# A decay table made by a scan on VectorE, fewer weight tiles decoded in the retention, and the first MLP outputs made tile by tile

## The chip, the cores and the metric

The kernel runs on one core of a Trainium2 chip. The metric is the device time of one execution in microseconds (us). TensorE, VectorE, ScalarE and GpSimd each run their own instruction list in order; the profile calls them PE (with PEld for its weight loads), DVE, ACT and POOL, and SP is the queue that issues most transfers.

## The reference, cut to what matters

Three layers run one after the other on a (2, 768, 512) activation, in float32. The MLP's weights arrive as 64-bit floats and must be decoded on the chip.

```python
# 1 retention: 8 heads of 64, blocks of 64 positions, a decay lam per head
Dmask = np.where(rel >= 0, lam[:, None, None] ** rel[None, :, :], 0.0)
intra = np.einsum('bhij,bhjd->bhid', np.einsum('bhic,bhjc->bhij', qb, kb) * Dmask[None], vb)
inter = np.einsum('bhid,bhde->bhie', qb * lam_pow[None], kv_state)
kv_state = lam_block * kv_state + np.einsum('bhsd,bhse->bhde', kb * rev_pow[None], vb)
# 2 MLP: layer norm, 512 -> 2048 -> 512, residual
xn = (x - mu) / np.sqrt(var + 1e-06) * g_ln
x = x + np.maximum(xn @ w_ch1, 0.0) @ w_ch2
# 3 attention with 4 experts, of which the gate takes 2
```

## The kernel before, in words

**Retention.** The main loop (L590) takes 12 chunks, n = 0 to 11, of 128 positions (two batches of six). Chunk n issues the scores of chunk n+1 (`ret_scores`, L322), the state products (`ret_state`, L352) and the inner products (`ret_inner`, L385). `ret_sum` (L363, L365) adds a state on DVE, twice per chunk (EARLY, then LATE), and POOL multiplies it by the decay (`old`, L375). `ret_decay` multiplies the next chunk's keys (`kd`, L337 on ACT, L338 on POOL) and scores (`a`, L341 on DVE) by the table `dec`. `ret_outer` (L402) adds the part that comes from the states, and `ret_copy` (L409) takes the chunk's result to `xT` on ACT. Scores and outputs share two large PSUM buffers (`ps_big`). Chunks with nothing else for PE run three dummy matmuls (`warm`, L100).

**The table.** `dec` is lam to the power i, for each head and position. Before, DVE makes the powers in six doublings on 8 partitions (L262), they go out to `zd` in DRAM and back in a shifted pattern to 64 partitions (L269), and ACT copies them to the other 64 (L270). The input loads of chunks 1 and 2 are issued on SP behind these transfers.

**Decoding.** One weight tile (a 512 KB load, L121, with three buffers) takes seven DVE instructions of 128x512 (L204, L205, L209, L218, L219, L223, L226) and two on ACT (L200, L214), in six parts (`prep_parts`). Each part has a hand-set cost; `room(us)` issues parts until the costs reach the budget. In the retention `room` is called twice per chunk, with 1.7 and 2.0. It takes the layer norm's parts (`minus` L439 and `low` L445 of a block of 384 positions) before weight parts. The eight tiles of group 0 (four of w1, four of w2) are decoded there.

**MLP.** There are four blocks of 384 positions and four groups of four tiles. A `g1` step is 12 matmuls (L503) and leaves `h` through a relu on ACT (L515) and a subtraction on DVE (L516). A `g2` step is 24 matmuls (L530), half of a block's output for one group, and is added to `xT` on DVE (L535). `steps` is the order, written out by hand; five `g1` steps stand in the retention, one per chunk in n = 6 to 10. After chunk 11 the by-hand loop goes on for six rounds of two steps, up to step 17. From there `mlp_step` runs one step at a time, and a planner (`plan`) says before which step a tile of groups 1 to 3 is decoded: here one per two steps from step 12. `ln_e` (L462 on PE, L484 on DVE) scales a block before its `g2`. Attention follows the MLP.

Of the kernel before, what the change touches and what calls it, by code (L numbers as in the profile page):

```python
# [17 lines left out]
P = 128  # L18
# [26 lines left out]
FIRST = ((0, 0), (1, 0), (2, 0), (0, 1), (1, 1), (2, 1), (0, 2), (1, 2), (2, 2), (3, 0))  # L45
# [18 lines left out]
def model(ctx, tc, qkT, kv, lam, g_ln, w12, wat, out):  # L64
# [69 lines left out]

    steps = [("g1", 0, blk, f) for f, blk in FIRST]
    for blk in range(NBLK - 2):
        steps += [("g2", 0, blk, 0), ("g1", 0, blk + 1, GF - 1), ("g2", 0, blk, 1)]
    groups = [(g, blk) for g in range(NG) for blk in range(NBLK)]
    for n, gb in enumerate(groups):
        if n < NBLK - 2:  # L140
            continue
        steps.append(("g2", *gb, 0))
        if n + 1 < len(groups):
            steps += [("g1", *groups[n + 1], f) for f in range(2)]
        steps.append(("g2", *gb, 1))
        if n + 1 < len(groups):
            steps += [("g1", *groups[n + 1], f) for f in range(2, GF)]

    def used(ft, i):

        at_ = [n for n, (kind, g, _, f) in enumerate(steps)
               if kind == ("g1", "g2")[i] and g == ft // GF and (i == 1 or f == ft % GF)]
        return at_[0], at_[-1]
# [7 lines left out]
    while rest:  # L161
        for p in rest:
            ft, i = p
            old = ft - W_SLOTS[i][1]
            if used(ft, i)[0] - n <= LEAD and (old < 0 or used(old, i)[1] < n - 1):
                break
        else:
            p = None
        if p and n >= free_at:
            plan[n] = p  # L170
            rest.remove(p)
            free_at = n + APART
        n += 1
        assert n < len(steps), rest
# [15 lines left out]
    def prep_parts(ft, i):  # L190
# [17 lines left out]
        def top():  # L208
# [3 lines left out]
            pool, bufs = (wpool, few) if ft % many < few else (WPOOL2[0], many - few)  # L212
# [45 lines left out]
    nc.vector.memset(zt[:, :C - 1], 0.0)  # L258
    nc.vector.memset(zt[:, C - 1:C], 1.0)
    m = 1  # L260
    while m < C:
        nc.vector.tensor_scalar(zt[:, C + m:C + 2 * m], zt[:, C:C + m], zt[:, C + m - 1:C + m], None, ALU.mult)  # L262
        m *= 2
    zd = dram.tile([H, P], F32, tag="zd", name="zd")
    nc.sync.dma_start(zd, zt)
    ret_load(*order[0], 1)

    zv = zd[:, :]
    nc.sync.dma_start(dec[:C], bass.AP(tensor=zv.tensor, offset=zv.offset, ap=[[1, C], [P, H], [1, C]]))  # L269
    nc.scalar.copy(dec[C:], dec[:C])  # L270
# [195 lines left out]
    def ln_d(blk):  # L466
# [5 lines left out]
        std = lnp.tile([P, NTB], F32, tag="std", name=f"std{blk}")  # L472
# [17 lines left out]
    HS, LAST, HXT = {}, [], []  # L490

    EXTRA = FIRST[EARLY_STEPS:] + ((GF - 1, 1),)
    assert len(EXTRA) <= 2 * HX

    def g1(g, blk, f):
# [9 lines left out]
        if g == 0 and (f, blk) in EXTRA:  # L505
            n = EXTRA.index((f, blk))
            if n % 2 == 0:
                HXT.append(ap_.tile([P, 2, 1040], F32R, tag="wa", name=f"hx{n}"))
            h = HXT[n // 2][:, :, n % 2 * TB:(n % 2 + 1) * TB]
        else:  # L510
# [45 lines left out]
    def mlp_step():  # L556
# [4 lines left out]
        decode(1 if due else 0)  # L561
        f, args, leave = step()
# [4 lines left out]
    norm_parts, weight_parts = [], [part for p in first for part in prep_parts(*p)]  # L567
# [16 lines left out]
    del pieces[:len(first)]  # L584
    ret_scores(0)
# [3 lines left out]
    norm_at, n, early = [0] * NBLK, 0, 0  # L589
    while n < len(order) or min(norm_at) < 5 or norm_parts or weight_parts:  # L590
        if n < len(order):
            if n + 3 < len(order):
                ret_load(*order[n + 3])
            ret_scores(n + 1)
            ret_state(n)
            ret_inner(n)
            ret_sum(n, EARLY)
# [3 lines left out]
        for blk in range(NBLK):  # L601
            if n >= NTB * (blk + 1) and norm_at[blk] < 5 and not (norm_at[blk] == 2 and blk not in XN) \
                    and not (norm_at[blk] == 1 and blk > 0 and norm_at[blk - 1] < 3):
                norm_parts += (ln_a, ln_b, ln_c, ln_d, ln_e)[norm_at[blk]](blk) or []
                norm_at[blk] += 1
        leave = None
        if n < len(order):
            room(ROOM[0])
            ret_sum(n, LATE)
            if n >= MLP_FROM and early < EARLY_STEPS and step_ready():  # L610
                leave = step()[2]
                early += 1
# [8 lines left out]
            room(ROOM[1] - (0.6 if leave else 0.0))  # L621
# [319 lines left out]
```

## Time and profile before

| | us |
|---|---|
| median of three runs (499.32 to 501.76) | 499.38 |
| profiled execution, own time | 499.64 |
| its span, first to last instruction | 497.9 |
| TensorE busy in the span | 471.1 |
| VectorE busy | 345.8 |
| last `ret_outer` ends | 91.2 |
| last `g2` matmul ends | 358.3 |

The own time is 1.74 us more than the span. Mean granted TensorE clock over the span is 0.973 of full speed; the lower values all stand in the first 56 us.

### The profile page before, as it was taken

Reading aid. Unit: us, or ns where it says so; the run is one execution under the profiler, and the core shown is the slowest. Engines: PE = TensorE matmul, PEld = TensorE weight load, DVE = VectorE, ACT = ScalarE, POOL = GpSimd, SP = SyncE. Lnnn points to the kernel's source line nnn. Section 1 sums busy time; section 2 is a strip of 40 time slices with the busy share of each in tenths; the row PEclk is TensorE's granted clock in tenths of the full one; section 3 lists DMA queues with packets and bytes.
Section 4 is the critical chain, followed back from the end, with each engine's and each line's share of the span. In section 5 each row is a group of like instructions: output and inputs, shape, how many; then the busy total and the mean of one; then the engine's idle time right before and its main releaser. Section 6 shows DMA issues by size and latency. Waiting matters only on the chain.

```text
span 497.9 us, 10394 instructions
## 1 busy us (share of the span) xinstructions
PE 471.1 (95%) x4231; PEld 436.3 (88%) x4231; DVE 345.8 (69%) x719; ACT 199.2 (40%) x454; POOL 99.9 (20%) x146
## 2 busy tenths in 40 slices
PE   5867999899998999999999999999999999999996
PEld 2645787799998999999999999999998889898885
DVE  2899988752699556987278995544478786677663
ACT  2335555441143122232122351221156666647672
POOL 4566455000000000000000000000025535334340
PEclk9579799999999999999999999999999999999999
DMA  6965741100123202222012231000000000100111
GB/s 214 354 214 207 257 170 45 43 1 0 43 85 128 86 5 82 84 86 84 1 42 86 86 127 43 1 1 0 1 2 0 13 32 1 43 3 22 43 41 67
DMA packets 11295, 35.41 MB, mean 71 GB/s; under 512 B 1896, under 2 KB 2160, under 8 KB 11248
## 3 DMA queue, kind: packets, MB, share of 16 engines
q1 hardware_dynamic: 10928, 34.62, 19.9%
q8 instruction: 33, 0.54, 0.4%
q10 hardware_dynamic: 288, 0.14, 0.1%
q14 instruction: 14, 0.11, 0.1%
q0 software_dynamic: 32, 0.00, 0.0%
HBM read 31.60 MB, written 3.15 MB: 70 GB/s over the span
## 4 chain that ended last, share of the span: by engine, by line
PE 76%; DVE 16%; ACT 3%; issue 2%; DMA 2%; POOL 0%; SPq 0%; DVEq 0%; ACTq 0%
PE y L530 25%; PE h L503 24%; PE pj L699 4%; PE s L779 4%; PE av L828 4%; PE o L849 3%; PE t L816 3%; PE pv L721 3%; DVE mag L204 2%; DVE w L226 1%; DVE top L223 1%; DVE xn L445 1%; DVE st L365 1%; DMA qk<-in_qkT 1%; DVE top L209 1%
## 5 line engine op out<-in xcount | busy, mean ns | idle before, releaser
L503 PE MATMUL h<-xn,w 128*128 128x384 f32 x768 | 140.9, 337 | 0.0
L503 PEld LDWEIGHTS h<-xn,w 128*128 128x128 f32 x768 | 133.3, 188 | 3.3 <-issue 2.5
L530 PE MATMUL y<-hs,w 128*128 128x384 f32 x696 | 126.2, 335 | 2.6 <-DVE hs L516 2.6
L530 PEld LDWEIGHTS y<-hs,w 128*128 128x128 f32 x696 | 121.0, 188 | 2.9 <-DVE hs L516 2.9
L515 ACT ACTIVATE hs<-h 128x384 fp32r<-128x384 f32 x58 | 28.5, 491 | 115.5 <-PE h L503 95.1
L713 POOL TENSOR_SCALAR kh<-kh 64x384 fp32r<-64x384 f32 x16 | 8.4, 525 | 292.6 <-DVE qs L707 281.0
L516 DVE SCALAR_TENSOR_TENSOR hs<-h,hs 128x384 fp32r<-128x384 f32 x58 | 32.2, 555 | 46.6 <-ACT hs L515 46.5
L535 DVE TENSOR_TENSOR xT<-xT,y 128x768 f32<-128x768 f32 x32 | 30.5, 952 | 39.5 <-PE y L530 39.5
L806 POOL TENSOR_SCALAR att<-att,c,gw 128x128 f32<-128x128 f32 (+5 forms) x48 | 35.8, 751 | 51.5 <-DVE c L803 16.3
L214 ACT CAST w<-top 128x512 fp32r<-128x512 f32 x32 | 19.9, 621 | 55.3 <-DVE top L209 55.3
L699 PE MATMUL pj<-x,wa 128*128 128x384 f32 x192 | 35.0, 337 | 0.0
L699 PEld LDWEIGHTS pj<-x,wa 128*128 128x128 f32 x192 | 33.4, 188 | 0.0
L817 ACT COPY aT<-t 128x512 f32<-128x512 f32 (+3 forms) x64 | 26.5, 442 | 11.1 <-PE t L816 10.8
L816 PE MATMUL t<-ident,att 128*128 128x128 f32 x168 | 26.2, 275 | 0.4 <-DVE qs L707 0.4
L226 DVE TENSOR_TENSOR w<-top,mag 128x512 fp32r<-128x512 f32 x32 | 23.4, 732 | 0.5
L828 PE MATMUL av<-aT,v 128*64 128x128 f32 x336 | 23.6, 280 | 0.0
L779 PE MATMUL s<-kh,qs 128*128 128x512 f32 (+3 forms) x64 | 23.2, 365 | 0.0
L219 DVE SCALAR_TENSOR_TENSOR mag<-raw,mag 128x512 f32<-128x512 uint32 x32 | 22.5, 703 | 0.8
L209 DVE SCALAR_TENSOR_TENSOR top<-raw,mag 128x512 int32<-128x512 int32 x32 | 22.4, 701 | 0.6
L223 DVE TENSOR_TENSOR top<-top,w 128x512 f32<-128x512 f32 x32 | 22.7, 711 | 0.0
L402 PEld LDWEIGHTS po<-qd,st 64*64 64x64 f32 x352 | 13.1, 153 | 10.9 <-issue 7.7
L200 ACT ACTIVATE mag<-raw 128x512 f32<-128x512 f32 x32 | 21.4, 669 | 1.1 <-DVE w L226 0.4
(119 smaller groups left out, 692.5 us busy)
## 6 DMA issues: line engine op xcount, KB each, us to landing
raw<-in_w SPq DMA_DIRECT2D x32, 512.0 KB, 3.7
qk<-in_qkT SPq DMA_DIRECT2D x12, 512.0 KB, 4.5
kvn<-in_kv SPq DMA_DIRECT2D x12, 512.0 KB, 4.8
out<-os SPq DMA_DIRECT2D x11, 256.0 KB, 2.0
rawa<-in_wat SPq DMA_DIRECT2D x3, 512.0 KB, 3.2
rawa<-in_wat SPq DMA_DIRECT2D x1, 520.0 KB, 4.2
dec<-zd SPq DMA_DIRECT2D x1, 128.0 KB, 4.9
out<-os SPq DMA_DIRECT2D x1, 128.0 KB
```

The source lines that it names most:

```text
L223: nc.vector.tensor_tensor(t["top"], t["top"], t["w"][:, 0].bitcast(F32), ALU.subtract)
L226: nc.vector.tensor_tensor(t["w"][:, 1], t["top"], t["mag"], ALU.add)
L503: nc.tensor.matmul(ph[:, :TB], w[:, wi, k, :], xn[:, xi, k, :], start=(i == 0), stop=(i == 11))
L515: LAST.append((nc.scalar.activation(h[:, 0], ph[:, :TB], AF.Relu), nc.vector.scalar_tensor_tensor(h[:, 1], ph[:, :TB], 0.0, h[:, 0].bitcas ...
L516: nc.vector.scalar_tensor_tensor(h[:, 1], ph[:, :TB], 0.0, h[:, 0].bitcast(F32), ALU.max, ALU.subtract)))
L530: nc.tensor.matmul(y[:, j, :TB], w[:, wi, e * P:(e + 1) * P], h[:, xi], start=(f == 0 and i == 0), stop=(f == GF - 1 and i == 2))
L535: nc.vector.tensor_tensor(xv, xv, y[:, :, :TB], ALU.add)
L699: nc.tensor.matmul(ps[:, :TB], w[:, wi, k, :], x2[:, xi, k, :], start=(i == 0), stop=(i == 11))
L779: nc.tensor.matmul(ps[:, c0:c1], q, kk[:, e, c0:c1], start=(i == 0), stop=(i == 1))
L806: nc.gpsimd.tensor_scalar(a[:, :n], a[:, :n], c, gw, ALU.mult, ALU.mult)
L816: nc.tensor.transpose(pt[:, (j - j0) * P:(j - j0 + 1) * P], a[:, j * P:(j + 1) * P], ident)
L828: nc.tensor.matmul(pav[e2 * HD:(e2 + 1) * HD, pr * P:(pr + 1) * P], v[:, j, e * HD:(e + 1) * HD], row["aT"][e][:, j * P:(j + 1) * P], star ...
```

## The change

- **Table.** `lq` (lam on all partitions) is loaded on SP ahead of all else. POOL makes a pattern of ones (`hit`), DVE copies it to `one`, copies `lq` to `mul`, zeroes the first column and runs one `tensor_tensor_scan` (multiply, add) over 128x512, which is `dec`. The doublings, `zd`, the transfer back and ACT's copy go. POOL's order of the first instructions is now also the written one.
- **Retention.** In chunk 0 nothing is decoded and `ret_scores(1)` stands behind `ret_inner(0)`. The budgets are 0.7 and 0.9 without a step and 1.4 and 1.6 with one. Only the w1 tiles of group 0 are in the list; the w2 tiles (`later_parts`) are appended after chunk 11, with the scaling of block 0 ahead of the last. `warm` runs in n = 0 to 4; a step may stand from n = 5 on. Worked through, the readiness rules give: no dummy and no step in n = 5 and 6, a `g1` step in each of n = 7 to 11.
- **Steps.** `next_step` takes the first ready of the steps in `FIRST`. After `FIRST` block 0's output is made by four `g2f` steps (12 matmuls, one w2 tile each, both large PSUM buffers), with `g1` of block 3 between them. Ten `g1` steps of group 1 stand ahead of group 1's first `g2` (step 36). There are 98 steps, 96 before.
- **Buffers and plan.** Early `h` tiles are put into free w1 slots of w2 (`IN_W`), `wa` buffers and the `dq` buffer. Planned decoding begins at step 20, one tile before each of steps 20 to 27, then 33, 34, 38 and on.
- **Scaling of blocks 1 to 3** (`ln_e`) is issued just ahead of each block's first `g2`.

```diff
-WARM = (10, 5)
-ROOM = (1.7, 2.0)
-ROOM_MLP = 1.6
-EARLY_STEPS = 5
-MLP_FROM = 6
-PLAN_FROM = 12
-LEAD = 12
+WARM = (8, 3)
+ROOM = ((0.7, 0.9), (1.4, 1.6))
+ROOM_MLP = 1.5
+MLP_FROM = 5
+PLAN_FROM = 20
+LEAD = 16
 APART = 2
+APART_FROM = 34
+FIRST = ((0, 0), (1, 0), (0, 1), (1, 1), (2, 0), (2, 1), (0, 2), (1, 2), (2, 2), (3, 0), (3, 1), (3, 2))
...
     steps = [("g1", 0, blk, f) for f, blk in FIRST]
-    for blk in range(NBLK - 2):
-        steps += [("g2", 0, blk, 0), ("g1", 0, blk + 1, GF - 1), ("g2", 0, blk, 1)]
+    for f in range(GF):
+        steps += [("g2f", 0, 0, f), ("g1", 0, NBLK - 1, f)]
...
+        half = len(more) // 2
+        steps += [("g2", *gb, 0)] + more[:half] + [("g2", *gb, 1)] + more[half:]
+        if gb == (0, NBLK - 1):
+            steps += [("g1", 1, 1, f) for f in range(GF)] + [("g1", 1, 2, f) for f in range(2)]
...
-    nc.sync.dma_start(zt[:, C:C + 1], lam)
-    nc.scalar.dma_start(lq, lam.rearrange("h o -> o h").to_broadcast([P, H]))
-    ret_load(*order[0], 0)
+    nc.sync.dma_start(lq, lam.rearrange("h o -> o h").to_broadcast([P, H]))
+    ret_load(*order[0])
...
-        nc.vector.tensor_scalar(zt[:, C + m:C + 2 * m], zt[:, C:C + m], zt[:, C + m - 1:C + m], None, ALU.mult)
-    nc.sync.dma_start(zd, zt)
-    ret_load(*order[0], 1)
-    nc.sync.dma_start(dec[:C], bass.AP(tensor=zv.tensor, offset=zv.offset, ap=[[1, C], [P, H], [1, C]]))
-    nc.scalar.copy(dec[C:], dec[:C])
+    nc.gpsimd.memset(hit, 0.0)
+    for a2 in range(2):
+        nc.gpsimd.affine_select(hit, hit, [[1, C]], ALU.not_equal, 1.0, base=1 - C * (a2 + 1), channel_multiplier=1)
+    nc.vector.tensor_copy(one, hit[:, None, :].to_broadcast([P, H, C]))
+    nc.vector.tensor_copy(mul, lq[:, :, None].to_broadcast([P, H, C]))
+    nc.vector.memset(mul[:, :, 0:1], 0.0)
+    nc.vector.tensor_tensor_scan(dec.rearrange("p h i -> p (h i)"), mul.rearrange("p h i -> p (h i)"),
+                                 one.rearrange("p h i -> p (h i)"), 0.0, ALU.mult, ALU.add)
...
+    def g2f(g, blk, f):
+        if f == 0:
+            YF.extend(ps_big(f"yf{j}") for j in range(2))
+        for e in range(KT):
+            for i, (wi, xi) in enumerate(PASSES):
+                nc.tensor.matmul(YF[e // 2][:, e % 2, :TB], w[:, wi, e * P:(e + 1) * P], h[:, xi],
+                                 start=(f == 0 and i == 0), stop=(f == GF - 1 and i == 2))
+        def leave():
+            if f == GF - 1:
+                for j in range(2):
+                    nc.vector.tensor_tensor(xv, xv, YF[j][:, :, :TB], ALU.add)
...
+            if todo[0] == ("g2", 0, blk, 0):
+                for _, scale in ln_e(blk):
+                    scale()
...
-    norm_parts, weight_parts = [], [part for p in first for part in prep_parts(*p)]
+    weight_parts = [part for ft in range(GF) for part in prep_parts(ft, 0)]
+    for ft in range(GF):
+        if ft == GF - 1:
+            later_parts.append((2.0, lambda: [f() for _, f in ln_e(0)]))
+        later_parts += prep_parts(ft, 1)
...
-            ret_scores(n + 1)
+            SCK[n + 1] = ps_big(f"sck{n + 1}")
+            if n > 0:
+                ret_scores(n + 1)
             ret_state(n)
             ret_inner(n)
+            if n == 0:
+                ret_scores(n + 1)
...
-            room(ROOM[0])
+            leave, early = None, ROOM[0]
+            if n >= MLP_FROM and any(ready(k, True) for k in range(len(FIRST) - len(steps) + len(todo))):
+                early = ROOM[1]
+            if n > 0:
+                room(early[0])
             ret_sum(n, LATE)
-            if n >= MLP_FROM and early < EARLY_STEPS and step_ready():
-                leave = step()[2]
-                early += 1
+            if early is ROOM[1]:
+                leave = next_step(True)
             elif n < MLP_FROM:
                 warm(3, f"c{n}")
```

## Rows read from the trace of the kernel before

**Rows 1.** The page, part 1: busy time, share of the span and instructions.

```profile
PE 471.1 (95%) x4231; PEld 436.3 (88%) x4231; DVE 345.8 (69%) x719; ACT 199.2 (40%) x454; POOL 99.9 (20%) x146
```

**Rows 2.** Windows cut at the EARLY sums: stretch, length, busy by engine, clock, DMA.

```profile
14.47:22.41 7.94, 6.13 (x118) 4.02 (x116) 7.73 (x12) 2.79 (x7) 4.16 (x4) 0.50 0.95 379
22.41:29.42 7.01, 4.60 (x133) 3.33 (x131) 6.87 (x11) 2.51 (x6) 4.43 (x4) 0.86 0.68 228
...
50.59:55.58 4.99, 4.55 (x133) 4.34 (x136) 4.85 (x11) 2.49 (x6) 1.21 (x1) 0.56 0.71 253
55.58:62.38 6.80, 6.80 (x149) 5.40 (x141) 6.23 (x11) 4.56 (x9) 3.62 (x4) 1.00 0.76 278
...
91.22:126.51 35.29, 35.29 (x219) 32.93 (x220) 17.51 (x29) 10.34 (x21) 0.00 (x0) 1.00 0.05 16
126.51:160.00 33.49, 30.89 (x179) 30.57 (x178) 29.03 (x58) 11.46 (x20) 0.00 (x0) 1.00 0.28 94
160.00:358.29 198.29, 198.29 (x1152) 198.29 (x1151) 128.36 (x212) 50.68 (x93) 0.00 (x0) 1.00 0.15 51
```

**Rows 3.** Timeline, first 15 us: start, length, engine, line, what, idle before and releaser.

```profile
3.66 0.43 POOL L280 COPY qpow<-lq 64x4 f32<-64x4 f32 x2 [0.78 <-DMA lq<-in_lam]
...
10.24 0.62 ACT L270 COPY dec<-dec 64x512 f32<-64x512 f32 x1 [7.60 <-DMA dec<-zd]
...
10.94 0.73 POOL L338 TENSOR_TENSOR kd<-kvn,dec 128x320 f32<-128x320 f32 x1 [4.43 <-ACT dec L270]
...
12.47 1.08 PE L352 MATMUL sck<-kvn,kd 64*64 64x64 f32 x32
...
14.47 0.42 DVE L363 COPY st<-sck 128x256 f32<-128x256 f32 x1 [2.89 <-PE po L385]
```

**Rows 4.** Timeline of chunks 1 to 3, 25 to 38 us.

```profile
25.39 0.69 PE L322 MATMUL sck<-qk 64*64 64x64 f32 x32 [0.68 <-ACT xT L409]
...
29.98 1.15 PE L402 MATMUL po<-qd,st 64*64 64x64 f32 x32 [2.22 <-DVE st L365]
...
31.64 0.58 ACT L409 COPY xT<-po 128x512 f32<-128x512 f32 x1
...
32.27 1.13 PE L322 MATMUL sck<-qk 64*64 64x64 f32 x32 [1.14 <-ACT xT L409]
...
34.03 1.08 PE L385 MATMUL po<-a,kvn 64*64 64x64 f32 x32
...
36.48 1.46 PE L100 MATMUL warmc<-zeros 128*128 128x512 bf16 x3
```

**Rows 5.** Groups of DVE instructions from 100 to 345 us.

```profile
L516 DVE SCALAR_TENSOR_TENSOR hs<-h,hs 128x384 fp32r<-128x384 f32 x51 | 28.3, 556 | 43.0 <-ACT hs L515 42.9
L535 DVE TENSOR_TENSOR xT<-xT,y 128x768 f32<-128x768 f32 x29 | 27.6, 952 | 31.3 <-PE y L530 31.3
L219 DVE SCALAR_TENSOR_TENSOR mag<-raw,mag 128x512 f32<-128x512 uint32 x24 | 16.6, 690 | 0.5
...
L205 DVE TENSOR_SCALAR mag<-mag 128x512 int32<-128x512 int32 x24 | 10.2, 424 | 0.4
```

**Rows 6.** One decode line in the retention (15 to 92 us): minimum/median/maximum ns.

```profile
L204 DVE TENSOR_SCALAR mag<-mag x8: 420/1482/1491, 15.4 to 80.5; 128x512 f32<-128x512 f32 x8
```

**Rows 7.** Timeline, 145 to 157 us: PE's wait in the MLP.

```profile
150.77 0.55 DVE L516 SCALAR_TENSOR_TENSOR hs<-h,hs 128x384 fp32r<-128x384 f32 x1
...
151.38 0.97 PE L530 MATMUL y<-hs,w 128*128 128x384 f32 x4 [2.60 <-DVE hs L516]
...
152.18 4.32 PE L503 MATMUL h<-xn,w 128*128 128x384 f32 x24
...
156.34 4.32 PE L530 MATMUL y<-hs,w 128*128 128x384 f32 x24
```

**Rows 8.** The chain that ended last, two pieces after the retention: start, length, what.

```profile
109.57 0.78 PE va L419 x8
...
123.75 0.67 PE sb L462 x6
```

More of the change, by code (lines that the diff above doesn't have):

```diff
@@ L135, in model @@
     steps = [("g1", 0, blk, f) for f, blk in FIRST]
-    for blk in range(NBLK - 2):
-        steps += [("g2", 0, blk, 0), ("g1", 0, blk + 1, GF - 1), ("g2", 0, blk, 1)]
+    for f in range(GF):
+        steps += [("g2f", 0, 0, f), ("g1", 0, NBLK - 1, f)]
     groups = [(g, blk) for g in range(NG) for blk in range(NBLK)]
     for n, gb in enumerate(groups):
-        if n < NBLK - 2:
+        if n == 0:
             continue
[L142 to L147, printed above, removed]
+        more = []
+        if n >= NBLK - 1 and n + 1 < len(groups):
+            more = [("g1", *groups[n + 1], f) for f in range(GF)]
+        if gb == (1, 0):
+            more = [("g1", 1, 2, f) for f in range(2, GF)]
+        elif gb == (1, 1):
+            more = []
+        half = len(more) // 2
+        steps += [("g2", *gb, 0)] + more[:half] + [("g2", *gb, 1)] + more[half:]
+        if gb == (0, NBLK - 1):
+            steps += [("g1", 1, 1, f) for f in range(GF)] + [("g1", 1, 2, f) for f in range(2)]
+    assert len(set(steps)) == len(steps)
     def used(ft, i):
         at_ = [n for n, (kind, g, _, f) in enumerate(steps)
-               if kind == ("g1", "g2")[i] and g == ft // GF and (i == 1 or f == ft % GF)]
+               if g == ft // GF and (kind == "g2" and i == 1 or kind == ("g1", "g2f")[i] and f == ft % GF)]
         return at_[0], at_[-1]
@@ L164, in model @@
             old = ft - W_SLOTS[i][1]
-            if used(ft, i)[0] - n <= LEAD and (old < 0 or used(old, i)[1] < n - 1):
+            free = used(old, i)[1] if old >= 0 else steps.index(("g2", 0, ft // 2 - 1, 1)) if i == 1 else 0
+            if used(ft, i)[0] - n <= LEAD and free < n - 1:
                 break
@@ L489, in model @@
     PASSES = ((0, 0), (1, 0), (0, 1))
-    HS, LAST, HXT = {}, [], []
-    EXTRA = FIRST[EARLY_STEPS:] + ((GF - 1, 1),)
-    assert len(EXTRA) <= 2 * HX
+    HS, LAST, HXT, HDQ = {}, [], [], []
     def g1(g, blk, f):
@@ L504, in g1 @@
                 i += 1
-        if g == 0 and (f, blk) in EXTRA:
-            n = EXTRA.index((f, blk))
+        if g == 0 and (f, blk) in IN_W:
+            h = wpool.tile([P, 2, 512], F32R, tag="w1", name=f"hw{f}_{blk}", bufs=W_SLOTS[1][0])[:, :, :TB]
+        elif (ft, blk) in IN_WA:
+            n = IN_WA.index((ft, blk))
             if n % 2 == 0:
@@ L509, in g1 @@
             h = HXT[n // 2][:, :, n % 2 * TB:(n % 2 + 1) * TB]
+        elif (ft, blk) in IN_DQ:
+            n = IN_DQ.index((ft, blk))
+            if n == 0:
+                HDQ.append(xnp.tile([P, 2, KT, TB], F32R, tag="dq", name="hdq", bufs=1))
+            h = HDQ[0][:, :, n]
         else:
@@ L561, in mlp_step @@
         decode(1 if due else 0)
+        for blk in range(1, NBLK):
+            if todo[0] == ("g2", 0, blk, 0):
+                for _, scale in ln_e(blk):
+                    scale()
         f, args, leave = step()
@@ L573, in room, with ready, next_step @@
             us -= cost
-    def step_ready():
-        f, g, blk, k = todo[0]
+    def ready(k, inside):
+        f, g, blk, j = todo[k]
         if f == "g1":
-            return blk in XN and (g * GF + k, 0) in W
-        return blk in SCALED and all((g * GF + j, 1) in W for j in range(GF))
+            return blk in XN and (g * GF + j, 0) in W and not (inside and (j, blk) in IN_WA)
+        return f == "g2f" and (g * GF + j, 1) in W and (j < GF - 1 or blk in SCALED) and not inside
+    def next_step(inside):
+        for k in range(max(1, len(FIRST) - len(steps) + len(todo))):
+            if ready(k, inside):
+                return step(k)[2]
+        return None
     by_hand = ExitStack()
@@ L620, in model @@
             ret_copy(n)
-            room(ROOM[1] - (0.6 if leave else 0.0))
+            if n > 0:
+                room(early[1])
         if n == len(order) - 1:
```

54 lines of the change are left out of this document (30 added, 24 removed).

## The prediction

> **What bounds the kernel now.** I read the page first. TensorE is busy for 95% of the span [rows 1], which looks like a kernel with nothing left but matmuls. An average hides stages, so next I cut the span at the places where `ret_sum` closes a chunk [rows 2]. From 91.22 us to the last `g2` at 358.29 PE is busy for all but the 2.60 us of one wait (35.29 of 35.29, 30.89 of 33.49, 198.29 of 198.29): that stage is bound by PE. The retention is another matter. There DVE is busy for nearly all of a chunk (7.73 of 7.94, 6.87 of 7.01), PE for some two thirds, and PE's busy time contains dummies and matmuls at a lowered clock (0.50 in one chunk, 0.56 in another, 1.00 from 55.58 on). So the retention is as long as DVE's list. Five `g1` steps stand in it, before and after the change. Whatever shortens it therefore pulls the whole PE-bound stage forward, unless DVE then fails to keep up behind it.
>
> The timeline of the start [rows 3] shows the other wait: lam is on all partitions at 3.66, but ACT waits 7.60 us for `dec` to come back from DRAM, POOL's `kd` starts at 10.94 and the first sum at 14.47.
>
> **The change, part by part.** Times before are those of the profiled execution (499.64 us, which is 0.26 above the median of 499.38).
>
> *Start.* The trace has no scan. Its nearest row is a DVE instruction of 128x512, 0.69 [rows 5]; far off on the other side is the same width held up by another engine, 1.49 [rows 6]. I take 1.0, and 0.5 and 0.1 for the copy of lam and the zeroing, so the table stands at 3.7 + 1.6 = 5.3 (4.9 to 5.8). POOL's three small pattern instructions lie in its wait for lam. The table is then not what comes last: SP now issues the loads without a wait between them, and they run one behind the other. The busiest chunk moved 379 GB/s [rows 2], so 512 KB take 1.4 us. Counted from lam's landing at 3.7, the first keys land at 5.1, the first values at 6.5, then chunk 1 at 7.9 and 9.3, one weight load, and chunk 2's keys at 12.1. `kd` takes 0.73 from 6.5, state and inner products 2.0 (12.47 to 14.47), so the first sum is at 9.2, 5.3 us earlier [rows 3]. The second needs chunk 2's keys, at 12.1, and three PE groups of 2.84 (32.27 to 35.11 at the lowered clock [rows 4]): 14.9, where it was 22.41. **Term 1: -7.5.** Bounds: -5.3 if the second sum wins nothing over the first, -10.0 if lam does not hold up the loads (1.4) and the three groups take 1.7, by the 0.69 against 1.13 of one of them [rows 4].
>
> *Chunks 1 to 6.* From 22.41 to 62.38 before: 39.97, or 6.66 each, set by DVE [rows 2]. A tile is four DVE instructions of 0.69 and three of 0.42, 4.0, and 4.2 with the gaps [rows 5]; beside POOL it costs more, as one of them took 1.48 there against 0.42 [rows 6]. The new budgets leave about half a tile or half a block's norm per chunk. With the table's product (as wide as those 0.69) and two sums of 0.42 [rows 3] DVE has 3.5 to 5.1 of work. Then the chain through PE matters: dummies (the sum hidden behind them), `ret_outer`, ACT's copy, three PE groups. At the lowered clock this is 1.46 + 1.15 + 0.65 + 2.84 = 6.1, with the dummies and the three groups at the full one 0.73 + 1.15 + 0.65 + 1.7 = 4.2 [rows 4]. I take 5.1, between them and near the one chunk of before in which DVE was not held up by POOL, 4.99 at a clock of 0.56 [rows 2]: 30.6. **Term 2: -9.4**, bounds -3.4 (6.1) and -14.6 (4.2).
>
> *Chunks 7 to 11.* In 7 to 10 DVE has the two normalized blocks as before, and the decode that stands beside them is about what scaling and decode were. I put nothing for these four, within 3 either way. In chunk 11 a `g1` step of 2.08 (half of 4.16 from 152.18 to 156.34 [rows 7]) now stands in front of `ret_outer`; the step it replaces stood in chunk 6, whose time is already in term 2. **Term 3: +1.7.** The retention then ends at 91.2 - 15.2 = 76.0.
>
> *Scaling of blocks 0 and 1* leaves the retention: 2 x 0.67 of PE [rows 8] move into the PE-bound stage. **Term 4: +1.3.** `g2f` has as many matmuls as the two `g2` halves that it replaces; its two additions are the old ones.
>
> *Decode moved behind the retention.* Four w2 tiles leave it, and the planned tiles come one per step at 20 to 27 where it was one per two. I added both engines up from the end of `ret_outer(11)` to step 36, the first that needs group 1's w2. PE: 25 steps of 12 matmuls x 2.08 = 52.0 (seven left of `FIRST`, four of block 3, four `g2f`, ten of group 1), six of 24 x 4.16 = 25.0 [rows 7], four scalings x 0.67 = 2.7, six pieces of the norms at about 0.7 = 4.3 [rows 8]: 84.0. DVE: twelve tiles x 4.2 = 50.4, 21 subtractions x 0.56 = 11.8, eight additions and eight scalings x 0.95 = 15.2, a block's norm 2 x 0.95 + 4 x 0.56 = 4.1 [rows 5]: 81.5. So DVE may idle for 2.5 us; each further one is a wait of PE. Before, the same two engines stood at 30.89 and 29.03 of 33.49, and PE waited 2.60 [rows 2]: a subtraction stood behind decoding in DVE's list until 150.77, and the `g2` that needed it came at 151.38 [rows 7]. Right behind the retention DVE will wait for relus of steps that PE has still to do; I estimate 7.5 us of idle time up to step 36, so 5.0 of waits in place of 2.6. **Term 5: +2.4**, bounds -2.6 (no wait is left) and +9.
>
> The sum: -7.5 - 9.4 + 1.7 + 1.3 + 2.4 = -11.5, so 488.1, or 487.9 beside the median. Forecast 488.
>
> What is costed at nothing: SP no longer waits between its first loads, and no later load is late, since chunk 4's is issued two chunks ahead and a chunk and a half of weight moves 1.5 MB in 5 us, under the 379 GB/s of before. Steps 36 to 53 have 54 of PE against 48 of DVE by the same prices, so no wait grows there. Attention is untouched.
>
> **The rivals.** *The clock stays low.* PE's clock fell to 0.50 and 0.56 in chunks in which it was busy for 77% and 91% with short groups [rows 2], and the change drops the dummies in chunks 5 and 6. If chunks 1 to 6 run at 6.1 and the first `g1` step takes twice its 2.08: 499.6 - 7.5 - 3.4 + 1.7 + 1.3 + 2.4 + 2.1 = 496. Against it: a shorter chunk holds the same matmuls, so PE idles less. The Trainium skill (TensorE: Matmul & The Clock Gate, "HAM oscillation") says that waits between groups of matmuls can put the clock back to half each time; the low chunks here agree, and by that rule alone this rival's 496 would stand. Chance 0.14.
>
> *POOL takes DVE's place.* POOL is busy 4.43 of a chunk of 7.01, waits for DVE's sums in between, and none of its work goes [rows 2]. If it holds chunks 1 to 6 at 6.66, only the start is won: 499.6 - 7.5 + 5.4 = 497.5. Against it: 1.21 of POOL in the chunk of 4.99 (the batch's last, which has less for it), and 3.62 in chunk 6 [rows 2]. Chance 0.08.
>
> *Slower: DVE becomes the bound of steps 20 to 27.* There DVE has eight tiles, six additions, two subtractions and three scalings, 46.1, against 31.2 of PE. If the two large PSUM buffers, which come free only by DVE's additions, let PE run no further ahead, 14.9 are lost and not made good, on top of the 5.0: 499.6 - 13.9 + 19.9 - 2.6 = 503. It decides from a wait of 16.5 us on. For it: DVE's list is fixed, and it has put decoding ahead of a subtraction before [rows 7]. Against it: steps 28 to 35 need only 4.5 of DVE for 16.6 of PE, so most of a backlog is worked off. Chance 0.06.
>
> *Better:* the full clock in chunks 1 to 6 and no waits behind them, 499.6 - 7.5 - 14.6 + 3.0 - 2.6 = 478. Chance 0.14. That the change does not do what it says is no case here: the table's wait goes with the transfer.
>
> **How the numbers follow.** The forecast, 483 to 494, has 0.58. The range, 480 to 496.5, takes in the clock rival and the upper half of the better case; left out are the other half of that (0.06), POOL's and the slower case (0.14). A measurement of this kernel tells no difference under 0.5%, 2.5 us. Faster: 0.58 + 0.14 + 0.14 = 0.86; within: POOL's 0.08; slower: 0.06.
>
> **What would show it.** The first sum near 9, the second near 15; sums some 5 us apart in chunks 1 to 6; `ret_outer(11)` at 76; from there to the last `g2` 271 us, with PE waiting some 5 us for DVE between steps 20 and 36; attention 139.6 as before. The prediction is wrong if the chunks' pitch stays above 6, if loads of chunk 2 or 3 land late, or if PE waits more than 12 us behind the retention.

## The result, and the profile after

The changed kernel takes 487.97 us in the median (485.91 to 489.12), beside 500.2 for the kernel before in the same comparison: ratio 0.9748 [0.9701, 0.9794]. The forecast was 488.0 in 480 to 496.5. The profiled execution has a span of 486.8, 11.1 less than before. Its total is what was forecast; most of its terms are not.

The page of the changed kernel, part 1 (it answers to [rows 1]) and the queue from part 3 that brings the instructions (packets, MB, share):

```profile
PE 465.2 (96%) x4219; PEld 432.4 (89%) x4224; DVE 337.4 (69%) x715; ACT 198.0 (41%) x453; POOL 99.4 (20%) x149
...
q8 instruction: 33, 0.54, 0.5%
```

The changed kernel in windows, as in [rows 2]: chunk 0 from its first sum on, three of chunks 1 to 6, chunks 1 to 6 and 7 to 11 in one row each, the stage behind the retention, attention.

```profile
12.09:16.68 4.59, 3.29 (x114) 2.30 (x115) 1.45 (x4) 1.86 (x5) 3.12 (x4) 1.00 1.02 413
16.68:23.77 7.09, 3.62 (x130) 2.94 (x131) 5.54 (x9) 1.93 (x5) 3.90 (x4) 0.98 0.60 222
23.77:31.30 7.53, 5.11 (x134) 4.02 (x137) 3.67 (x8) 1.87 (x5) 4.03 (x4) 0.73 0.77 271
41.40:44.86 3.46, 2.89 (x132) 2.73 (x136) 3.25 (x6) 2.87 (x7) 1.25 (x2) 1.00 0.82 240
...
16.68:50.47 33.79, 24.03 (x766) 17.94 (x772) 24.07 (x39) 14.68 (x36) 21.40 (x22) 0.90 0.67 234
50.47:81.23 30.76, 27.61 (x600) 23.44 (x596) 25.56 (x44) 18.45 (x39) 14.01 (x16) 1.00 0.32 106
81.23:346.90 265.67, 265.67 (x1558) 263.31 (x1559) 186.98 (x323) 76.12 (x141) 0.00 (x0) 1.00 0.18 58
346.90:486.80 139.90, 135.25 (x1053) 120.13 (x1051) 96.20 (x301) 83.72 (x224) 52.86 (x80) 1.00 0.07 24
```

In the retention DVE is no longer busy for nearly all of a chunk: 24.07 of 33.79, where [rows 2] had 6.87 of 7.01. No other engine has taken its place: PE has 24.03, POOL 21.40. A stretch in which nobody is full is set by a chain of waits. Behind the retention PE is busy without a break, 265.67 of 265.67; the wait in [rows 7] is gone.

Cut at the same places as the prediction's terms:

| term | predicted | measured |
|---|---|---|
| 1, start to second EARLY sum | 22.41 to 14.9, -7.5 | 22.41 to 16.68, -5.7 |
| 2, chunks 1 to 6 | 39.97 to 30.6, -9.4 | 39.97 to 33.79, -6.2 |
| 3, chunks 7 to 11 | +1.7 | 28.84 to 30.76, +1.9 |
| 4 and 5, stage behind the retention | +3.7 | 267.07 to 265.67, -1.4 |
| attention | 0 | 139.61 to 139.90, +0.3 |
| sum | -11.5 | -11.1 |

The retention ends 5 us later than forecast (81.2, not 76.0), and the stage behind it is 5 us shorter. The experiments ask for the reason of each.

The timeline of the start, as in [rows 3]:

```profile
3.54 0.43 POOL L295 COPY qpow<-lq 64x4 f32<-64x4 f32 x2 [1.21 <-DMA lq<-in_lam]
...
4.62 0.58 DVE L281 COPY one<-hit 128x512 f32<-128x512 f32 x1 [3.48 <-POOL hit L280]
...
5.70 1.22 DVE L284 TENSOR_TENSOR_SCAN dec<-mul,one 128x512 f32<-128x512 f32 x1
...
8.42 0.73 POOL L352 TENSOR_TENSOR kd<-kvn,dec 128x320 f32<-128x320 f32 x1
...
12.09 0.42 DVE L377 COPY st<-sck 128x256 f32<-128x256 f32 x1 [4.37 <-PE sck L336]
```

The table stands at 6.92 (5.70 + 1.22), not 5.3: DVE waited for the pattern of ones (`hit`), whose last piece POOL made at 4.34, behind its copies of lam and two constants. POOL's part of `kd` of chunk 0 begins only at 8.42, since POOL works through its constants (identity, mask, powers) first. The first sum then waits for the scores of chunk 1, which the change puts behind `ret_inner(0)` and which are written into the same PSUM buffer: 12.09, not 9.2.

The timeline of PE in chunks 0 and 1 shows what the forecast did not know of:

```profile
14.30 0.66 PE L366 MATMUL sck<-kvn,kd 64*64 64x64 f32 x31
15.84 0.21 PE L366 MATMUL sck<-kvn,kd 64*64 64x64 f32 x1 [0.88 <-issue]
...
19.87 0.63 PE L366 MATMUL sck<-kvn,kd 64*64 64x64 f32 x27
22.85 0.28 PE L366 MATMUL sck<-kvn,kd 64*64 64x64 f32 x3 [2.35 <-issue]
```

PE stops inside a run of 32 equal matmuls, and what ends the wait is "issue", that is, the profile shows nothing that it waited for. The view of waits, PE from 14 to 50 us (what, total, times, longest), finds five of them:

```profile
PE sck L366 <- issue: 7.5, 5, 2.4
```

That is more than any other wait of PE there (the next is 1.0). The first of the five, 0.9, lies before the second EARLY sum, the other 6.6 in chunks 1 to 6. The kernel before has none inside a group of equal matmuls in this stretch. The places have a rule. 33 packets of 0.54 MB on the instruction queue are 16 KB each; PE's 8443 instructions (4219 matmuls, 4224 weight loads) over 33 packets are 256 for each, 64 bytes an instruction, if that queue is PE's. The first gap stands after 221 matmuls, the second 127 further on, the third some 125: 256 instructions, half of them matmuls. And the DMA view of 20 to 22 us, ahead of the second gap's end, has one such packet:

```profile
q8 instruction: 1, 0.02, 3.4%
```

### The profile page after: what moved, and what is told of

Its sections match the earlier page's. It is cut to its first block, busy times and chain, and to the rows that moved or that the text cites. A ratio compares the mean times of both kernels' runs of the same rounds, so it can differ in the third digit from the quotient of the medians.

```text
span 486.8 us, 10377 instructions
## 1 busy us (share of the span) xinstructions
PE 465.2 (96%) x4219; PEld 432.4 (89%) x4224; DVE 337.4 (69%) x715; ACT 198.0 (41%) x453; POOL 99.4 (20%) x149
## 4 chain that ended last, share of the span: by engine, by line
PE 84%; DVE 7%; ACT 3%; issue 3%; POOL 1%; DMA 1%; DVEq 0%; POOLq 0%; ACTq 0%
PE h L513 26%; PE y L547 26%; PE pj L764 4%; PE s L844 4%; PE av L893 4%; PE o L914 4%; PE t L881 4%; PE pv L786 3%; PE yf L566 2%; PE po L416 2%; PE sck L366 1%; PE po L399 1%; PE sck L336 1%; ACT xn L455 1%; PE warmc L106 1%
## 5 line engine op out<-in xcount | busy, mean ns | idle before, releaser
L547 PE MATMUL y<-hs,w 128*128 128x384 f32 x552 | 99.8, 334 | 0.0
L547 PEld LDWEIGHTS y<-hs,w 128*128 128x128 f32 x552 | 96.1, 188 | 0.0
L532 ACT ACTIVATE hs<-h 128x384 fp32r<-128x384 f32 x50 | 24.5, 490 | 103.5 <-PE h L513 90.0
L533 DVE SCALAR_TENSOR_TENSOR hs<-h,hs 128x384 fp32r<-128x384 f32 x50 | 27.7, 555 | 42.5 <-ACT hs L532 42.5
L552 DVE TENSOR_TENSOR xT<-xT,y 128x768 f32<-128x768 f32 x30 | 28.5, 950 | 31.6 <-PE y L547 31.6
L893 PEld LDWEIGHTS av<-aT,v 128*64 128x64 f32 x336 | 17.8, 136 | 4.4 <-issue 3.9
```

Source lines behind the costliest of these rows:

```text
L532: LAST.append((nc.scalar.activation(h[:, 0], ph[:, :TB], AF.Relu), nc.vector.scalar_tensor_tensor(h[:, 1], ph[:, :TB], 0.0, h[:, 0].bitcas ...
L533: nc.vector.scalar_tensor_tensor(h[:, 1], ph[:, :TB], 0.0, h[:, 0].bitcast(F32), ALU.max, ALU.subtract)))
L547: nc.tensor.matmul(y[:, j, :TB], w[:, wi, e * P:(e + 1) * P], h[:, xi], start=(f == 0 and i == 0), stop=(f == GF - 1 and i == 2))
L552: nc.vector.tensor_tensor(xv, xv, y[:, :, :TB], ALU.add)
L893: nc.tensor.matmul(pav[e2 * HD:(e2 + 1) * HD, pr * P:(pr + 1) * P], v[:, j, e * HD:(e + 1) * HD], row["aT"][e][:, j * P:(j + 1) * P], star ...
```

## The experiments

**The table alone, and all but the table.** `e1_table` is the kernel before with the new table; `e2_oldtable` is the changed kernel with the old one.

```diff
-    zd = dram.tile([H, P], F32, tag="zd", name="zd")
-    nc.sync.dma_start(zd, zt)
...
+    nc.vector.tensor_tensor_scan(dec.rearrange("p h i -> p (h i)"), mul.rearrange("p h i -> p (h i)"),
+                                 one.rearrange("p h i -> p (h i)"), 0.0, ALU.mult, ALU.add)
```

> The kernel before with only the new table (lam loaded first on SP, pattern of ones, scan); budgets, steps and decode as before. Theory DVE (the retention is DVE's list, so a start that is earlier is won whole): first sum near 11 to 12 in place of 14.5, chunk pitch 7.0 as before, all of it kept to the end: 4 to 6 us less, 494 to 496. Rival (the earlier start runs into transfers or into PE's own waits in chunks 1 to 3): 0 to 2 us less. If it wins 10 or more, the table is the whole change.

> The changed kernel with the old table (doublings, DRAM and back); everything else as changed. If the parts add up: 4 to 6 us more than the changed kernel, 492 to 494, the second sum near 21 to 22. Rival (the loads behind the table's transfers come later and leave PE's waits in chunks 1 to 3 fewer, so that part of the loss comes back): 1 to 3 us more.

`e1_table`: 496.08 (495.6 to 500.63), ratio 0.9956 [0.9931, 0.9981]. Its first sum comes at 10.48 (14.47 before) and the last at 85.03 (89.51), so in the profiled execution the earlier start is kept whole, as the theory had it, and the own time is 495.6 against 499.64. Over all executions it is less. `e2_oldtable`: 487.37 (487.11 to 490.29), 0.9773 [0.9732, 0.9814], which can't be told from the changed kernel; its second EARLY sum is at 18.03 and its last at 78.16 (16.68 and 79.24 with the scan). So the table is worth some 2 us where the rest is as before (0.9 to 3.4 by the interval; 4.0 in the profiled execution), and nothing that can be measured in the changed kernel. A row of `e1_table` after its start, from one LATE sum to the next, shows the old pitch:

```profile
14.60:21.61 7.01, 5.04 (x130) 3.92 (x131) 6.86 (x11) 2.67 (x8) 4.43 (x4) 0.58 0.96 364
```

DVE is busy for 6.86 of 7.01, as in [rows 2].

**Budgets of before.** `e3_budgets` gives DVE its old share of decoding in every chunk.

```diff
-ROOM = ((0.7, 0.9), (1.4, 1.6))
+ROOM = ((1.7, 2.0), (1.7, 2.0))
```

> The changed kernel with the decode budgets of before (1.7 and 2.0 in every chunk); the list of tiles stays the four of w1. Theory DVE (the budgets set the pitch of chunks 1 to 6): their pitch goes from 5.6 back to 6.5 or 7, 4 to 8 us more. Theory PE's instructions (chunks 1 to 3 are held by gaps in which PE waits for nothing in the trace, at every 127th matmul or so): chunks 1 to 3 stay at 7.0 to 7.5, and the kernel is within 2 us of the changed one, since DVE had room in these chunks (3.7 to 5.5 busy of 7.1 to 7.5).

490.82 (490.33 to 492.07), 0.9832 [0.9799, 0.9866]. Chunks 1 to 6 took 39.3, as in the kernel before; chunks 7 to 10 took 24.9 instead of 28.8, since less was left to decode. So 3.9 of the 5.5 us that the old budgets cost come back, and the total is 2.9 more by the medians (4.2 by the ratios, 0.9832 against 0.9748), below or at the lower end of what was expected. Most of the gain of 12 us therefore doesn't hang on the budgets: this kernel, which like the changed one decodes only four tiles in the retention, keeps 8 of it. Two of the chunks in windows:

```profile
24.57:31.82 7.25, 5.22 (x132) 4.83 (x136) 6.96 (x12) 2.48 (x6) 4.42 (x4) 0.50 0.63 221
38.85:46.01 7.16, 5.72 (x124) 4.55 (x124) 7.07 (x11) 4.80 (x10) 5.14 (x6) 0.95 0.46 161
```

The budgets are what makes chunks 3 and 4 short: with the old ones they take 7.03 and 7.16 (5.28 and 4.82 in the changed kernel), DVE is full again (7.07 of 7.16), and the pitch is 7 at either clock. But chunk 2 takes 7.25 here and 7.53 in the changed kernel, in which DVE does half the work. Something else holds that chunk there.

**Is it the instruction blocks?** `e5_shift` puts 40 more short dummies ahead of chunk 0. If a gap belongs to what PE waits for, it stays at its instruction; if it belongs to a place in PE's list, it moves 40 matmuls back.

```diff
     warm(WARM[1], "b")
+    ps40 = ps_mid("shift")
+    for _ in range(40):
+        nc.tensor.matmul(ps40[:, :32], zeros[:, :P], zeros[:, :32], start=True, stop=True)
```

> The changed kernel with 40 more small dummy matmuls (32 columns of zeros) behind the dummies after the first scores. Theory PE's instructions (each gap stands where a block of 256 PE instructions ends, 128 matmuls with their weight loads): the gaps move 40 matmuls earlier in PE's list, out of the state products: the first one from the end of the state products of chunk 1 to the scores or the outer products before them, the next likewise one chunk on. Rival (the gap belongs to the state products, for data that the trace doesn't name): the gaps stay in the state products. Time: within 2 us.

A single execution, 489.78. The timeline of its PE at the first gap:

```profile
12.62 0.58 PE L336 MATMUL sck<-qk 64*64 64x64 f32 x24 [0.39 <-DVE st L379]
...
15.32 0.49 PE L336 MATMUL sck<-qk 64*64 64x64 f32 x8 [2.12 <-issue]
```

The gap has left the state products (after 31 of 32) and stands in the scores ahead of them (after 24 of 32): 39 matmuls earlier. It follows the place in the list, and the view of waits now has four of them in the scores, 6.6 us. So PE stops at a place in its list, and by the count of packets that place is the end of a block of its instructions.

**Loads out of the way.** In the changed kernel the first three weight tiles (512 KB each) are issued among the first loads of keys and values (from 3.06 us on). `e4_lateloads` issues them one per chunk.

```diff
-    load_next()
     ret_load(*order[2])
-    load_next(2)
...
+            if n < 3:
+                load_next()
```

> The changed kernel with its first three weight loads issued one per chunk in chunks 0 to 2, not among the first loads. Theory backlog (PE's instruction blocks of 16 KB come late because they wait behind bulk loads): the gaps of 2.35 and 2.2 us in chunks 2 and 3 fall below 1, sums of chunks 2 to 4 come 2 to 4 us earlier, 2 to 4 us less. Rival (a block takes its time whatever else moves): the gaps stay at 2 or more, within 1 us, or slower if the first weight tile is then late.

483.49 (482.92 to 483.8), 0.9678 [0.9641, 0.9715]: 4.5 us under the changed kernel (fastest 485.91) by the medians of two comparisons, 3.5 by their ratios. The second sum comes at 15.60, the last EARLY sum at 74.42 (79.24). The stage behind is the same, 265.65. Waits of PE from 14 to 50 us, and chunks 1 to 6 as a window:

```profile
PE sck L334 <- issue: 2.9, 1, 2.9
PE sck L364 <- issue: 1.2, 2, 0.9
...
15.60:46.26 30.66, 23.74 (x772) 18.23 (x775) 25.02 (x39) 15.44 (x38) 21.58 (x23) 0.94 0.80 288
```

These waits fall from 7.5 to 4.1 us, and chunks 1 to 6 from 33.8 to 30.7. But only 1.2 of the 4.1 lie inside a group of equal matmuls. The other stands ahead of a whole group, and three rows of the timeline tell more of it:

```profile
18.19 0.66 ACT L216 ACTIVATE mag<-raw 128x512 f32<-128x512 f32 x1 [2.90 <-DMA raw<-in_w]
...
19.69 0.42 DVE L377 TENSOR_TENSOR st<-sck,old 128x256 f32<-128x256 f32 x1
...
20.21 1.13 PE L334 MATMUL sck<-qk 64*64 64x64 f32 x32 [2.89 <-issue]
```

ACT waits for the first weight tile, which now lands late; DVE's LATE sum stands behind that tile's first parts; and PE goes on 0.10 us after the end of that sum, as it does in all three other kernels below with late loads and dummies, and in the changed kernel, where the profile names the sum. This looks like the price of the later load and not like the end of a block. It isn't shown: in `e10_nodummies` these scores start ahead of that sum (18.23 and 18.53), and no run takes the two apart.

The size is uncertain by an execution's scatter: in three other kernels with the same retention as the changed one (`e6_halves`, `e7_extra1`, `e7_extra2`), chunks 1 to 6 took 31.5 to 32.2 and the last EARLY sum came at 76.3 to 77.0, and in the later `e9_consts`, with late loads, they took 33.6. The stops inside groups set the two kinds apart better: from 14 to 50 us they come to 5.3 to 7.5 us in the changed kernel and those three, and to 1.2 to 3.5 in the four with late loads and dummies (`e4_lateloads`, `e8_late_oldtable` and the two `e9` kernels). How the loads delay the blocks (by the DMA engines, or by memory) was not tried.

**The table once more.** `e8_late_oldtable` is `e4_lateloads` with the old table.

> The changed kernel with the first weight loads one per chunk and the old table. Theory backlog (what the new table wins at the first sum is lost behind the loads that it lets go early): with those loads out of the way the old table costs 2 to 4 us against the kernel with late loads and the new table (483.5), 485.5 to 487.5. Rival (chunks 1 to 3 are paced by PE's instruction blocks, so the start is worth nothing): within 1 us of 483.5.

487.12 (484.92 to 487.95), 0.971 [0.964, 0.9779]; last EARLY sum at 77.55. It was 483.49 and 74.42 with the scan, in another comparison; `e9_consts`, run beside it, is the same but for POOL's order and took 484.16. So the scan is worth about 3 us once the start has no loads in its way; the intervals overlap, so that the size is not firm.

**The rest of the start.** `e9_consts` is `e4_lateloads` with POOL's constants behind the first chunk's `kd` and `qd`; `e9b_consts_scores` also puts chunk 1's scores ahead of chunk 0's state products.

```diff
-    sum_w = const.tile([P, 32], F32, tag="sumw", name="sum_w")
...
     ret_qd(*order[0])
+    sum_w = const.tile([P, 32], F32, tag="sumw", name="sum_w")
...
-            if n > 0:
-                ret_scores(n + 1)
+            ret_scores(n + 1)
             ret_state(n)
             ret_inner(n)
-            if n == 0:
-                ret_scores(n + 1)
```

> Late loads, and POOL makes the identity, the mask and four more constants behind the first chunk's keys, not ahead of them. In the changed kernel POOL starts these keys at 8.42, 1.5 us behind the table; theory POOL: they start near 7, the first sum comes 1 to 1.5 us earlier and 0.5 to 1.5 us are left at the end. Rival (chunk 1's and 2's loads or PE's instruction blocks set the second sum): under 0.5 us.

> The same, and chunk 1's scores stand ahead of chunk 0's state products again, as before the change. In the changed kernel the first sum waited for these scores, which write the same buffer. Theory: they now run while PE waits for the keys, the first sum comes about 1 us earlier than in the run beside it, time 0 to 1 us less. Rival (chunk 1's keys land later than chunk 0's keys are made): 1 to 2 us more.

484.16 (483.56 to 485.76) and 484.47 (483.83 to 487.95), against 483.49: nothing won. The first sum does come earlier, at 10.66 and then at 9.80 (12.15 in `e4_lateloads`), so both causes of its delay were the right ones. The second EARLY sum comes at 14.57 and 14.61 (15.60), and the last at 76.34 and 75.09, no earlier than 74.42. In the profiled executions the lead was lost on the way: `e9b_consts_scores` still had 1.4 us of it at the EARLY sum of chunk 5 (35.41 against 36.85) and then lost 2.05 in one stop inside a group, where `e4_lateloads` lost 0.95.

**The dummies.** `e10_nodummies` is `e4_lateloads` without them in chunks 0 to 4.

```diff
             elif n < MLP_FROM:
-                warm(3, f"c{n}")
+                pass
```

> Late loads without the three dummies in chunks 0 to 4. Theory chain (the dummies stand between inner and outer products in PE's list, 0.7 to 1.5 us per chunk): chunks 1 to 4 get 0.5 us shorter each, 1 to 3 us less. Rival clock (without them PE's granted clock falls to a half in these chunks and the groups take 2.8 in place of 1.7): 2 to 5 us more, with a granted clock under 0.9 between 15 and 40 us.

487.4 (486.03 to 490.37), 0.9733 [0.9669, 0.9796], some 3 us more than `e9_consts` beside it, and each of its executions was slower than each of that one. Windows of 16 to 40 us, `e4_lateloads`, then this one, then `e9_consts`:

```profile
16.00:40.00 24.00, 18.08 (x596) 14.58 (x597) 19.13 (x32) 12.13 (x29) 17.20 (x18) 0.93 0.85 303
```

```profile
16.00:40.00 24.00, 17.45 (x603) 14.53 (x604) 18.91 (x30) 11.84 (x28) 17.17 (x18) 0.86 0.84 287
```

```profile
16.00:40.00 24.00, 18.77 (x575) 14.59 (x571) 17.95 (x30) 12.36 (x29) 16.04 (x17) 0.86 0.86 295
```

The total is in the rival's range, but its reason is not shown. The granted clock is 0.86 instead of 0.93, yet `e9_consts`, with all its dummies, has 0.86 too. And the chunks without dummies lost nothing in the profiled execution: the EARLY sum of chunk 6 came at 41.05 (41.28 in `e4_lateloads`). The 4 us came in chunks 6 and 7, which have no dummies in either kernel: the first holds a stop of 3.05 inside a group of inner products, and the second ran at a granted clock of 0.85 (1.00). Why the dummies are worth 3 us, and whether it is by the clock or by where the blocks of instructions end, stays open.

**Outputs of block 0 in halves.** `e6_halves` takes `g2f` back: block 0's output in two `g2` steps, which need all four w2 tiles at once.

```diff
-    for f in range(GF):
-        steps += [("g2f", 0, 0, f), ("g1", 0, NBLK - 1, f)]
+    steps += [("g2", 0, 0, 0), ("g1", 0, NBLK - 1, 0), ("g2", 0, 0, 1)]
+    steps += [("g1", 0, NBLK - 1, f) for f in range(1, GF)]
```

> The changed kernel with block 0's first output made as two halves that need all four w2 tiles (as before the change), in place of four steps of one tile each. Theory (PE would stand still until the fourth w2 tile is decoded): by the trace of the changed kernel the fourth tile is ready some 31 us after the retention, and PE has about 18 us of steps that need none: 8 to 14 us more. Rival (DVE catches up since nothing else is in its list): under 3 us more.

498.59 (495.55 to 499.9), 0.9984 [0.9962, 1.0006]: the whole gain is gone. In the profiled execution, one of 495.88, the stage behind the retention takes 275.2 (+9.5). Waits of PE from 75 to 360 us:

```profile
PE y L547 <- ACT w L231: 3.1, 2, 2.8
PE y L547 <- DVE w L243: 2.7, 2, 1.5
```

5.8 us are waits for w2 tiles. The windows also show a lowered clock, such as 0.84 from 100 to 110 us and 0.82 from 110 to 120, where PE is busy throughout (some 1.8 us by that clock); how the rest of the other 3.7 is made up was not settled.

**How much slack has DVE behind the retention?** `e7_extra1` makes the last addition of a tile (0.6 us) twice in the 12 tiles decoded between the retention and step 36, `e7_extra2` three times. The output stays the same.

```diff
-            nc.vector.tensor_tensor(t["w"][:, 1], t["top"], t["mag"], ALU.add)
+            for _ in range(1 + 1 * ((i == 1 and ft < GF) or GF <= ft < 2 * GF)):
+                nc.vector.tensor_tensor(t["w"][:, 1], t["top"], t["mag"], ALU.add)
```

> The changed kernel with one DVE instruction of 128x512 more (the last addition made twice) in each of the twelve tiles decoded between the retention and step 36. Theory slack (a decode instruction costs its start-to-start distance of 0.60, not its 0.69, so DVE was done 6 us ahead of step 36): 7.2 us more of DVE, 0 to 2 us more of time. Rival (DVE is at its limit there, as my ledger had it): all of it shows, 6 to 8 us more.

> The same with two more in each of the twelve tiles, 14.4 us of DVE. Theory slack: the slack of some 6 us and part of the idle time are used up, 4 to 9 us more, with PE waiting for DVE between steps 20 and 36. Rival (no slack): 13 to 16 us more. If it is under 2, DVE is far from its limit there.

494.9 (494.04 to 498.95), 0.9941 [0.9904, 0.9978], and 504.74 (504.02 to 508.66), 1.0131 [1.0083, 1.0179]. The stage grows by 8.7 for 7.2 us of DVE, and by 17.7 for 14.4. The slack theory falls: there is next to none. Waits of PE from 75 to 360 us and two windows of `e7_extra1`:

```profile
PE h L514 <- DVE hs L534: 3.0, 1, 3.0
PE yf L567 <- DVE w L244: 1.9, 1, 1.9
...
110.00:125.00 15.00, 13.11 (x69) 12.79 (x68) 10.43 (x19) 2.72 (x5) 0.00 (x0) 0.89 0.11 36
155.00:170.00 15.00, 12.01 (x61) 11.47 (x60) 13.25 (x27) 5.17 (x11) 0.00 (x0) 0.89 0.23 81
```

The waits are 4.9, and in the two stretches that hold them the clock is granted at 0.89 (1.00 without the extra work). An estimate from these rows: two stretches of 15 us at 0.89 lose 2 x 15 x 0.11 = 3.3, which with the waits is 8.2 of the 8.7. So here a wait cost more than its length. Not every wait does: the 2.60 of the kernel before lies in a stretch that has 1.00 throughout [rows 2].

## Why the prediction was right, and by which steps

The total was right by luck in its size: two mis-sized groups of terms cancelled, -5.7 - 6.2 where -7.5 - 9.4 stood, and -1.4 where +3.7 stood. What was right in the mechanism is that DVE's list set the length of the retention, that less of it shortens chunks (four of chunks 1 to 6; chunks 1 and 2 took 7.09 and 7.53, where both had 7.01), and that the stage behind stays bound by PE.

**Start: the mechanism was right, the size was not.** The step that failed is "so the first sum is at 9.2". It took POOL as free at 6.5 (it began `kd` at 8.42) and put nothing in front of the sum for the scores that the change moves there; with both mended (`e9b_consts_scores`) it is at 9.80. For the end this mattered little. The scan took 1.22, not 1.0, and "POOL's three small pattern instructions lie in its wait for lam" failed for the last of the three, which DVE waited for. The claim that the table is not what comes last holds in the changed kernel, with the old table no slower (`e2_oldtable`), but not for the reason given: what came last was POOL's list and the scores, not the loads. The second sum, forecast at 14.9, came at 16.68, after a stop of 0.88 that no term had.

**Chunks 1 to 6: the step that failed is "then the chain through PE matters: ... I take 5.1".** That DVE would stop setting the pitch is shown (`e3_budgets`, and 24.07 of 33.79). The chain was summed from PE's groups and the copy as if PE's instructions were always there. They were not for 6.6 us of these chunks in the profiled execution. The chunks took 5.6 instead of 5.1; with later weight loads 5.1 in the one execution that was profiled (`e4_lateloads`). The prediction excluded harm from loads by bandwidth ("under the 379 GB/s of before"). No load of keys or values was late by that, but the blocks of instructions come over DMA too.

**Chunks 7 to 11** came to +1.9 where +1.7 was forecast, and this too was luck. The prediction put nothing on chunks 7 to 10 and all of it on the `g1` step in chunk 11. Chunks 7 to 10 took 28.77 instead of 27.13, +1.6, and chunk 11 took 1.99 instead of 1.71, from its sum to the end of `ret_outer`, +0.3. Before, PE waited 1.10 there for DVE's sum and ran a scaling of 0.93; the `g1` step of 2.38 fills both places. The step that failed is pricing it as if it came on top.

```profile
89.51:91.22 1.71, 1.15 (x36) 1.11 (x40) 1.71 (x4) 0.00 (x0) 0.00 (x0) 1.00 0.04 10
```

```profile
79.24:81.23 1.99, 1.99 (x42) 1.67 (x44) 0.94 (x3) 0.49 (x1) 0.00 (x0) 1.00 0.03 8
```

**Scaling** cost about what it was priced at, as far as a difference of the whole stage tells: before without its wait is 267.07 - 2.60 = 264.47, and the stage now takes 265.67, +1.2 for +1.3.

**Decode behind the retention: the step that failed is the ledger of DVE, 81.5 of 84.0.** It was priced by the durations of single instructions in [rows 5]. The timeline of the changed kernel in the MLP:

```profile
108.94 0.69 DVE L225 SCALAR_TENSOR_TENSOR top<-raw,mag 128x512 int32<-128x512 int32 x1
...
109.67 0.43 DVE L235 TENSOR_SCALAR mag<-top 128x512 int32<-128x512 int32 x1
...
148.14 0.42 DVE L221 TENSOR_SCALAR mag<-mag 128x512 int32<-128x512 int32 x1
148.47 0.69 DVE L236 SCALAR_TENSOR_TENSOR mag<-raw,mag 128x512 f32<-128x512 uint32 x1
149.08 0.69 DVE L240 TENSOR_TENSOR top<-top,w 128x512 f32<-128x512 f32 x1
149.68 0.69 DVE L225 SCALAR_TENSOR_TENSOR top<-raw,mag 128x512 int32<-128x512 int32 x1
```

In the last four rows, where the parts of two tiles alternate, an instruction of 0.69 is followed after 0.60 and one of 0.42 after 0.33: neighbours overlap, and a list is as long as its starts. In the first two rows one tile is decoded alone, `mag` is made from the `top` of the instruction before, and nothing overlaps (0.73 for 0.69). By their starts the four w2 tiles of group 0 take about 3.9 each and the eight tiles of steps 20 to 27 about 3.4: 42.8, where the ledger has 12 x 4.2 = 50.4. DVE had 9.6 us without work up to 125 us, a little more than the 7.5 allowed, and no wait was left: DVE ended the last tile of w2 in group 1 at 159.2, and step 36 came at 165.65. So the term was -2.6, its lower bound.

**Where the ledger misled a second time.** Those 6.4 us look like slack, and `e7_extra1` shows that they aren't: what counts is each deadline on the way. The timeline of the changed kernel at the fourth w2 tile of group 0:

```profile
111.81 0.68 DVE L243 TENSOR_TENSOR w<-top,mag 128x512 fp32r<-128x512 f32 x1
...
113.58 2.24 PE L566 MATMUL yf<-hs,w 128*128 128x384 f32 x12
```

The tile is ready 1.1 us before its `g2f` (113.58 - 112.49). The other deadline is the buffers of `h`, by which PE in `e7_extra1` waited 3.0 us after eight extra additions of 0.6: 4.8 - 3.0, so about 1.8 us to spare by this estimate. `e6_halves` asks for that fourth tile earlier and pays 9.5. It is therefore `g2f` that makes the decode behind the retention free of waits, by little.

**The rivals.** *The clock stays low*: 0.90 over chunks 1 to 6, where before had 0.81 and single chunks of 0.50. At most it is 0.10 of PE's 24.03 us, 2.4 of a miss of 3.2; how much of that lies on the chain was not tried. The Trainium skill (TensorE: Matmul & The Clock Gate, "HAM oscillation") says that waits between groups of matmuls can put the clock back to half each time; `e7_extra1` agrees in part, with 0.89 where PE waited 1.9 and 3.0, and the kernel before does not, with 1.00 around its wait of 2.60. *POOL takes DVE's place*: no, 21.40 of 33.79. *DVE becomes the bound of steps 20 to 27*: not at these sizes, but 14.4 us more of DVE made the kernel slower than before (`e7_extra2`): its stage grew by 17.7, and the prediction put that point at a wait of 16.5.

**What stays open.** What in the loads delays a block of instructions, and how much of 7.5 us an average execution has (5.3 to 7.5 in four profiled ones). Why the kernel is 3 us slower without the dummies. And some 1.9 of the 9.5 us of `e6_halves`.

## What to carry to other kernels

Where a stretch is freed from its full engine, look in the trace for waits that "issue" ends: here they stood among short matmuls, of which a block of 256 instructions lasted some 5 to 7 us, and bulk loads at that time are better issued a few chunks later (3.5 to 4.5 us here), as long as nothing in an engine's list stands behind them. Look also at whether such a wait lies inside a group of equal instructions or ahead of one: the second can be a wait for another engine that the profile doesn't name. Price an engine's list by the distance between starts of neighbours, not by durations, and check a moved work's deadlines one by one: a sum of idle time over a long stretch said 6 us where the nearest deadline had 1. A gain at the first step of a chain is worth nothing until the step behind it can use it, so try it again after the next change: the table could not be measured here, and was worth some 3 us with later loads. And check each term of a sum against its own stretch: a term that comes out right, like that of chunks 7 to 11, can be right for another reason.

## What the runs showed of the hardware that was not expected

- PE's instructions arrive in blocks of 256 (16 KB) during the run, and PE can stand up to 2.4 us at the end of one, in the midst of equal matmuls (changed kernel; 3.05 in `e10_nodummies`).
- Single waits of 1.9 and 3.0 us in an otherwise full stream of matmuls brought the granted clock to 0.89 over the stretches of 15 us that held them (`e7_extra1`), and with 7.2 us of work added on DVE the stage grew by 8.7 although its waits were 4.9. A single wait of 2.60 in the kernel before left the clock at 1.00.
- Consecutive DVE instructions of 128x512 overlap by some 0.09 us each where one doesn't need the result of the one before, so that a tile's seven, 4.0 by their durations, take some 3.4 in a list in which two tiles alternate, and about 3.9 alone.
